# The values of group 6 loaded in two halves, its output rows multiplied ahead of group 7's values, and w4 with ten rows to a partition

## The chip, the cores and the metric

The kernel runs on one core of one Trainium2 chip. The metric is the device time of one execution in microseconds (us), lower being better, as the median of five runs. A profile of one further execution gives the durations of single instructions and the records of the data transfers. Times within the profile are counted from the start of its span.

## The reference, cut to what matters

One token (512 numbers) is normalised. One branch attends with 32 heads over the last 4096 positions of a cache of keys and values; the other is a small feed-forward block. The result is `x + s * g`.

```python
W = min(4096, max(256, Sk // 4))              # 4096
q = (xn @ wq).reshape(...)                    # 32 heads of 128
scores = einsum("bhqd,bhkd->bhqk", q, k[:, :, Sk - W:, :]) * Dh ** -0.5
o = einsum("bhqk,bhkd->bhqd", softmax(scores), v[:, :, Sk - W:, :])
s = o.reshape(1, 1, 32 * 128) @ wo            # wo: 4096 x 512
h2 = gelu(layernorm(x1) @ w3) @ w4            # w3: 512 x 1376, w4: 1376 x 512
g = silu(x1 + h2)                             # with one token the shifted h is zero
out = x + s * g
```

Keys and values of the window are 32 x 4096 x 128 bf16 each, 33.6 MB each; the weights add another 11.7 MB. Every byte is used once.

## The kernel before, in words

The heads are worked in NG = 8 groups of G = 4. A group's keys are one tile of 128 partitions x 128 positions x 128 numbers (4 MB, 32 KB to a partition, loaded by `load_kv` at L97), and its values are another. The main loop (L507) has ten steps. In step s the keys of group s are scored: part of the positions on VectorE (`k_vector`, L297: a product and a sum), the rest turned on TensorE, copied by ScalarE and multiplied on TensorE (`k_turn`, L313, and `k_scores`, L321). The softmax of group s - 1 is ended, and the values of group h = s - 2 are multiplied by its weights (`v_part`, L410, one small matmul for each of the 128 positions of a partition, L423). Steps 8 and 9 have no keys left: step 8 works on the values of group 6, step 9 on those of group 7.

All loads but the two of x are issued by SyncE in program order (`load`, L78). A key tile can be loaded once one of three key buffers is free, a value tile once one of two value buffers is free: the values of group 7 go to the buffer of group 5, and so wait for the multiplication of group 5 (in step 7). Each transfer reports on one of eight semaphores in turn, so that it also waits until the transfer eight before it has landed. On TensorE, VectorE and ScalarE the order in the loop is kept as it is written (`manual_schedule`, L503).

The rows of the output weight `wo` are used in three blocks. Heads 0 to 15 are multiplied in step 6 (`y_wide`), heads 16 to 23 in step 8 (`y_block(1)`). Of heads 24 to 31, which are groups 6 and 7, a first piece is gathered (`few`, block 2): the 20 x 2 rows of `wo_few` (loaded at L395, 160 KB twice) hold 320 of group 6's 512 rows, and need `ox_pick` and `ox_few`, a chain of two matmuls and three VectorE instructions after the values of group 6. The other rows lie in `wo_rows`, one head to a slot, and are multiplied by `y_head` (L498): heads 26 and 27 with group 6 (`h_part` = 26), heads 28 to 31 with group 7. `rows_add` (L147) issues four matmuls for each row column.

In the last step (s = 9, L518 to L522 and L590 to L599) SyncE issues the first rows of `wo_rows`, the values of group 7 in three pieces (positions 0 to 64, 64 to 112 and 112 to 128, `cuts` at L502), and the rows of heads 28 to 31 in three transfers. TensorE multiplies the first piece of group 7's values, then the few block and heads 26 and 27, then the other two pieces of values; VectorE scales the result (`v_out`, L442), TensorE multiplies heads 28 to 31, VectorE multiplies by g and adds x (L602, L604), and SyncE stores 1 KB (L605).

At the start, w4 (1376 rows) is loaded in three transfers (L91 to L93): rows 0 to 1023 with 8 rows to a partition, rows 1024 to 1279 with 2, and the last 96 with one. The columns of w3 that belong to a chunk of w4's rows are picked with the same step (`chunks`, L204 to L206, used at L210 and L221): step 8 for eight chunks, 2 for two chunks, 1 for the last.

## Time and profile before

| what | us |
|---|---|
| median of 5 runs | 194.5 (194.4, 194.5, 194.5, 194.59, 195.68) |
| the profiled execution, whole | 195.93 |
| its span | 194.0 |
| VectorE busy | 145.8 (75%) |
| TensorE matmuls busy | 133.5 (69%) |
| ScalarE busy | 86.0 (44%) |
| the 16 DMA engines, busy on SyncE's queue | 96.0% of the span |
| bytes read | 78.84 MB, 406 GB/s over the span |

The profile shows the busy time of each engine, the transfers by queue, the chain of work that ended last, and a timeline of instructions. A line of the timeline gives start, duration, engine, line of the kernel, operation, output and inputs with their shapes and count; in brackets stands how long the engine had been idle before, and what ended that. "SPq" is SyncE issuing transfers. PEld is TensorE loading weights, which runs beside its matmuls (PE). The granted TensorE clock was 0.67 of full speed in the mean over the span.

### The profile page before, as it was taken

How to read it: one execution, taken by the hardware profiler on the slowest of the kernel's cores; microseconds unless marked ns; L12 is line 12 of the kernel's file. 1: busy time of each engine (PE TensorE's matmuls, PEld its weight loads, DVE VectorE, ACT ScalarE, POOL GpSimd, SP SyncE). 2: the span in 40 equal slices, each digit the busy share in tenths (PEclk: the TensorE clock that was granted, in tenths of full speed). 3: DMA queues.
4: the chain of work that ended last, by engine and by line, in shares of the span. 5: the costliest groups of instructions: out<-in, count | busy, mean ns of one | idle time of the engine just before them, and what ended most of it. 6: DMA issues, size and time to landing. Idle time of an engine off the chain costs nothing.

```text
span 194.0 us, 4716 instructions
## 1 busy us (share of the span) xinstructions
PE 133.5 (69%) x2098; PEld 101.6 (52%) x2098; DVE 145.8 (75%) x160; ACT 86.0 (44%) x193; POOL 6.5 (3%) x14
## 2 busy tenths in 40 slices
PE   0549750987946469878686994981788878843792
PEld 0444540876835433467675444881668246832781
DVE  1540119986999999999999999996799999950201
ACT  2003010788788280367376304771385069740000
POOL 2110007000000000000000000000000000000000
PEclk9999965567575556995555599555555599855555
DMA  5999999999999999999999999999999999999980
GB/s 208 404 408 426 378 422 464 426 432 429 426 442 426 432 427 422 439 432 432 429 429 426 432 429 402 463 432 429 432 429 434 429 432 399 463 411 373 413 333 18
DMA packets 4869, 79.13 MB, mean 408 GB/s; under 512 B 682, under 2 KB 1482, under 8 KB 1866
## 3 DMA queue, kind: packets, MB, share of 16 engines
q1 hardware_dynamic: 4698, 78.84, 96.0%
q8 instruction: 16, 0.26, 0.6%
q10 hardware_dynamic: 152, 0.00, 0.0%
q14 instruction: 3, 0.02, 0.0%
HBM read 78.84 MB, written 0.00 MB: 406 GB/s over the span
## 4 chain that ended last, share of the span: by engine, by line
DVE 42%; DMA 38%; PE 11%; ACT 6%; issue 1%; SPq 0%; ACTq 0%
DMA kv<-in_A_k_cache_dram 27%; DVE S L303 25%; DVE prod L301 14%; DMA kv<-in_A_v_cache_dram 9%; ACT kt L319 5%; PE pt L317 3%; PE yr_ps L489 3%; PE oT L423 3%; DMA x_bf<-in_A_x_dram 2%; PE sT L325 1%; DVE S L339 1%; DVE m L341 1%; DVE mx L349 1%; ACT own L334 0%; SPq L79 0%
## 5 line engine op out<-in xcount | busy, mean ns | idle before, releaser
L303 DVE TENSOR_REDUCE S<-prod 128x20 f32<-128x2560 bf16 (+1 forms) x32 | 83.8, 2620 | 1.1
L319 ACT COPY kt<-pt 128x1024 bf16<-128x1024 bf16 x54 | 53.2, 1014 | 25.7 <-PE pt L317 25.0
L317 PE MATMUL pt<-ident_bf,kv 128*128 128x128 bf16 x432 | 46.2, 277 | 12.0 <-DMA kv<-in_A_k_cache_dram 10.3
L301 DVE TENSOR_TENSOR prod<-kv,q_bc 128x2560 bf16<-128x2560 bf16 (+1 forms) x32 | 44.3, 1386 | 5.6 <-DMA kv<-in_A_k_cache_dram 2.9
L317 PEld LDWEIGHTS <-kv 128*128 128x128 bf16 x432 | 37.1, 127 | 14.3 <-DMA kv<-in_A_k_cache_dram 10.7
L325 PE MATMUL sT<-qT_bf,kt 128*128 128x4 bf16 x432 | 20.1, 169 | 16.5 <-ACT kt L319 15.6
L325 PEld LDWEIGHTS <-kt 128*128 128x128 bf16 x432 | 16.9, 105 | 23.9 <-ACT kt L319 23.7
L423 PE MATMUL oT<-pT,kv 128*128 128x4 bf16 x768 | 21.5, 166 | 3.3 <-DMA kv<-in_A_v_cache_dram 3.1
L423 PEld LDWEIGHTS <-kv 128*128 128x128 bf16 x768 | 21.0, 103 | 5.1 <-DMA kv<-in_A_v_cache_dram 4.8
L415 PE MATMUL ov<-kv,pT 128*16 128x512 bf16 x64 | 18.6, 464 | 0.0
L363 ACT ACTIVATE pT<-S,mb 128x128 bf16<-128x128 f32 x32 | 13.9, 570 | 0.3
L415 PEld LDWEIGHTS <-pT 128*16 128x16 bf16 x64 | 6.6, 105 | 11.1 <-issue 6.3
L442 DVE TENSOR_TENSOR o<-oT,rden 128x4 bf16<-128x4 f32 x2 | 0.3, 163 | 13.8 <-PE oT L423 13.8
L334 ACT ACTIVATE own<-sT,par 128x48 f32<-128x48 f32 (+1 forms) x32 | 7.6, 359 | 3.7 <-PE sT L325 3.7
L363 ACT ACTIVATION_READ_ACCUMULATOR pT<-S,mb 128x1 f32 x32 | 8.2, 255 | 0.0
L446 ACT ACTIVATE o<-oT,rden 128x1 bf16<-128x1 f32 x24 | 4.3, 260 | 8.2 <-PE oT L430 4.6
L418 ACT COPY ov_sb<-ov 16x512 f32<-16x512 f32 x2 | 1.2, 576 | 14.6 <-PE ov L415 14.6
L224 DVE COPY hr<-hr_ps 1x512 f32<-1x512 f32 x1 | 0.7, 679 | 7.7 <-PE hr_ps L221 7.7
L356 PE MATMUL mb_ps<-md,par_t 5*128 5x4 f32 x16 | 4.2, 328 | 2.6 <-DVE md L351 1.9
L489 PE MATMUL yr_ps<-wo,ox 128*1 128x512 bf16 x16 | 5.3, 506 | 0.9 <-DVE ox L467 0.9
L347 PE MATMUL mt_ps<-ident_f,m 128*1 128x128 f32 x8 | 2.9, 360 | 3.8 <-DVE rden L374 3.8
L213 ACT ACTIVATE a_bf<-a_ps 128x10 bf16<-128x10 f32 x1 | 0.2, 180 | 11.9 <-PE a_ps L210 11.9
(113 smaller groups left out, 89.5 us busy)
## 6 DMA issues: line engine op xcount, KB each, us to landing
kv<-in_A_k_cache_dram SPq DMA_DIRECT2D x7, 4096.0 KB, 31.6
kv<-in_A_v_cache_dram SPq DMA_DIRECT2D x7, 4096.0 KB, 30.5
wq_sb<-in_A_wq_dram SPq DMA_DIRECT2D x1, 4096.0 KB, 19.0
kv<-in_A_k_cache_dram SPq DMA_DIRECT2D x2, 2048.0 KB, 24.0
wo<-in_A_wo_dram SPq DMA_DIRECT2D x1, 2048.0 KB, 30.5
kv<-in_A_v_cache_dram SPq DMA_DIRECT2D x1, 2048.0 KB, 14.0
kv<-in_A_v_cache_dram SPq DMA_DIRECT2D x1, 1536.0 KB, 17.0
w_sb<-in_B_w_dram SPq DMA_DIRECT2D x1, 1376.0 KB, 6.7
```

Of the source, the lines that this page charges most:

```text
L301: nc.vector.tensor_tensor(out=prod[:, 0:m, :], in0=kn[:, rows, :], in1=q_bc[:, g:g + 1, :].to_broadcast([P, m, Dh]), op=ALU.mult)
L303: nc.vector.tensor_reduce(out=st[g]["S"][:, rows], in_=prod[:, 0:m, :], axis=AX.X, op=ALU.add)
L317: nc.tensor.transpose(pt[:, c - c0, :], kn[:, c, :], ident_bf[:])
L319: nc.scalar.copy(out=kts[b][:, 0:c1 - c0, :], in_=pt[:, 0:c1 - c0, :])
L325: nc.tensor.matmul(st[g]["sT"][:, c - nd(g), :], lhsT=kt[:, c - c0, :], rhs=qT_bf[:, G * g:G * g + G], start=True, stop=True)
L334: nc.scalar.mul(s["own"][:, 0:m, a], s["sT"][:, 0:m, a], par[:, a:a + 1])
L356: nc.tensor.matmul(mb_ps[:], lhsT=par_t[:].rearrange("k b a -> k (b a)"), rhs=md[:], start=True, stop=True)
L363: nc.scalar.activation(out=s["pT"][:, :, a], in_=s["S"][:], func=ACT.Exp, scale=scale, bias=mb[:, a:a + 1], accum_out=s["sum"][:, a:a + 1])
L415: nc.tensor.matmul(s["ov"][:], lhsT=s["pT"][:, c:c + 4, :].rearrange("p i a -> p (i a)"), rhs=v[:, c:c + 4, :], start=(c == 0), stop=(c == ...
L423: nc.tensor.matmul(s["oT"][:], lhsT=v[:, c, :], rhs=s["pT"][:, c, :], start=(c == 0), stop=(c == CP - 1))
L446: nc.scalar.mul(o_blk[b][:, c + k:c + k + 1], st[g]["oT"][:, k:k + 1], st[g]["rden"][:, k:k + 1])
L489: nc.tensor.matmul(yr[i][:], lhsT=ox_blk[i][:, t:t + 1], rhs=wo_blk[i][:, t, :], start=(t == 0), stop=(t == n - 1))
```

## The change

The second half of the diff splits the load of the values of group 6 (h == NG - 2) into two transfers of 64 positions, 16 KB to a partition each, and puts the few block and heads 26 and 27 before the first piece of group 7's values on TensorE. The first half loads rows 0 to 1279 of w4 in one transfer of 10 rows (10 KB) to a partition instead of two of 8 and 2 rows, and picks w3's columns with step 10 accordingly. Nothing else is changed; the number of SyncE's transfers stays the same, one fewer at the start and one more near the end. Line numbers after L92 move up by one to three.

```diff
-    assert F == 8 * P + 2 * P + 96
+    assert F == 10 * P + 96
...
-    load(w4_sb[:, 0:8, :], B_w4[0:8 * P, :].rearrange("(p c) n -> p c n", p=P))
-    load(w4_sb[:, 8:10, :], B_w4[8 * P:10 * P, :].rearrange("(p c) n -> p c n", p=P))
+    load(w4_sb[:, 0:10, :], B_w4[0:10 * P, :].rearrange("(p c) n -> p c n", p=P))
     load(w4_sb[0:96, 10, :], B_w4[10 * P:F, :])
...
-    chunks = [(P, slice(r, 8 * P, 8)) for r in range(8)]
-    chunks += [(P, slice(8 * P + r, 10 * P, 2)) for r in range(2)]
+    chunks = [(P, slice(r, 10 * P, 10)) for r in range(10)]
     chunks += [(96, slice(10 * P, F, 1))]
...
         elif h >= 0:
-            v = load_kv(v_pool, A_v_cache, h)
+            v = load_kv(v_pool, A_v_cache, h, (0, 64, CP) if h == NG - 2 else (0, CP))
...
         else:
-            v_part(h, v, 0, cuts[1])
             y_block(few_block)
             for r in range(h_part, H - G):
                 y_head(r)
-            for c0, c1 in zip(cuts[1:], cuts[2:]):
+            for c0, c1 in zip(cuts, cuts[1:]):
                 v_part(h, v, c0, c1)
             v_out(h)
```

## The prediction

> **What bounds the kernel now.** I read the page's slices first, then the transfers by queue, then the end of the chain of waits, and last the timeline of the last 15 us.

> ```profile
> DVE  1540119986999999999999999996799999950201
> DMA  5999999999999999999999999999999999999980
> GB/s 208 404 408 426 378 422 464 426 432 429 426 442 426 432 427 422 439 432 432 429 429 426 432 429 402 463 432 429 432 429 434 429 432 399 463 411 373 413 333 18
> ...
> q1 hardware_dynamic: 4698, 78.84, 96.0%
> q8 instruction: 16, 0.26, 0.6%
> ```

> VectorE is 75% busy, but its nines end near slice 35 (170 us). The DMA row is at nine from the second slice to the last but one. From 33 to 170 us the windows view gives a DMA share of 1.00 and 430 GB/s. In the trace's records of single packets, 16 are in flight at nearly every sampled moment from 3 to 186 us. So the transfers are never short of issued work: the bound is 78.84 MB through 16 engines.

> ```profile
> 170.62 0.15 SPq L79
> 170.77 0.04 issue
> 170.82 16.99 DMA kv<-in_A_v_cache_dram
> 187.81 0.05 issue
> 187.85 1.88 PE oT L423 x64
> 189.73 0.02 issue
> 189.76 0.17 DVE o L442
> 189.93 0.04 issue
> 189.97 0.72 PE y_ps L150 x15
> ```

> The chain shows the end: the second piece of group 7's values lands at 187.81, 64 small matmuls follow, VectorE scales, heads 28 to 31 are multiplied. But it hides one wait. The records of landings put the last row of wo (head 31) at 190.34, and the single records of L150 show its four matmuls starting at 190.39. So the very last transfer releases the end; the chain through 187.81 ends at almost the same moment. After 190.39 there are 3.66 us of span: a matmul, two VectorE instructions, a store, the program's end.

> ```profile
> 174.20 1.02 PE L150 MATMUL y_ps<-wo,ox 128*1 128x128 bf16 x32 [0.62 <-DVE ox L467]
> 175.15 0.60 PE L150 MATMUL y_ps<-y_row,ones_f 1*1 1x128 f32 x8
> 178.86 3.58 PE L423 MATMUL oT<-pT,kv 128*128 128x4 bf16 x128 [3.11 <-DMA kv<-in_A_v_cache_dram]
> 184.17 0.16 DVE L476 CAST of<-of_ps 64x8 bf16<-64x8 f32 x1 [0.26 <-PE of_ps L473]
> 184.22 1.87 PE L423 MATMUL oT<-pT,kv 128*128 128x4 bf16 x64
> 186.02 1.02 PE L150 MATMUL y_ps<-wo_few,of 64*1 64x128 bf16 x32
> 187.85 1.87 PE L423 MATMUL oT<-pT,kv 128*128 128x4 bf16 x64
> 190.72 0.29 DVE L602 TENSOR_TENSOR y<-y_ps,g_row 128x128 f32<-128x128 f32 x1 [0.80 <-PE y_ps L150]
> ```

> To be seen here: TensorE waits for group 6's values until 178.86, for the first piece of group 7 until 184.22, and for the second until 187.85. Between these it has slack.

> [...] one row's landings spread from 186.5 to 190.34 us, and each half of `few` (20 partitions) has five data landings[...]. [...] q8 above has 16 such packets, of 1.00 to 1.14 us each[...].

> **The change part by part.**

> *Group 6 in halves.* The bytes stay; 128 packets of 32 KB become 256 of 16 KB. From the packet records: 32 KB takes 1.213 us at the median (1.228 mean), 16 KB 0.614 (0.637 with the instruction packets among them). Per engine 16 x 0.614 - 8 x 1.213 = +0.12 us at the medians; with both minima (0.611 and 1.213) +0.07. The dearest price the trace offers is that of group 7's first piece, 0.652 in its window: 16 x 0.652 - 8 x 1.229 = +0.60. Below zero there is no reason. I take +0.08, and it is on the path. SyncE issues one more transfer (0.53 to 0.6 us); queued behind it are two wo_rows loads and group 7's. These are not delayed, since group 7's issue waits for group 5's multiplication until 170.2, and the queue of work then lasts until 178.8, a cover of 8.6 us.

> TensorE's first half can start when it lands. The last engine gets there about 16 KB x 8 = 4.9 us before 178.8, so at 173.9; TensorE is free at 175.75. 64 matmuls at 27.3 ns end at 177.5, the second half runs from 178.9 to 180.7 instead of 182.4. `of` (184.33 before, 1.9 us after the last of these matmuls) is ready at 182.6. That is 1.7 us earlier, on a chain that nothing late waits for.

> *Output rows first.* The 32 + 8 matmuls (1.02 us and some 0.65 us) run from 182.6 to 184.3. The first piece of group 7, landed at 184.17, then runs 184.3 to 186.2. Next is the second piece, which lands at 187.81 plus the 0.08: TensorE idles 1.7 us instead of 0.36 and starts at the same moment. Gain zero: what was filled with row matmuls becomes a wait. If the halves brought nothing, `of` would stay at 184.33, the rows end at 186.1, the first piece at 188.0, and the 64 matmuls behind it at 189.8: 0.1 us late. In both orders the third piece (landed 189.03) is done by 189.8.

> *w4 in one transfer.* 8 KB takes 0.309 us, 2 KB 0.084, 11,008 bytes 0.413; 10 KB is not in the trace. Between 8 KB and 11,008 bytes it comes to 0.385: 8 x (0.385 - 0.393) = -0.07 us per engine. The ends are 8 x (0.413 - 0.393) = +0.16 and, at the 11,008-byte rate scaled, -0.07. I take -0.07. One issue less on SyncE (0.43 us) leaves all later ones earlier, which a full queue doesn't notice. The columns of w3 are picked with step 10 instead of 8 or 2: L210's weight loads take 103 to 311 ns, 44 of them. If all took 311, it would be 13.7 us instead of 2.6. Even these 11 us would hide: SyncE would issue the first values at some 40 instead of 28.7 us, when two groups of keys are in the queue until 52.9. The first keys would be scored later by up to 6 us, and the transfers behind have covers of 8.6 us and more. I take zero.

> *Waits by turn.* The transfer eight places before has to have landed before the next is issued. The shifted count changes the partners. The second half of group 6 waits for group 6's keys (landed 136.8), a wo_rows load for group 7's keys (156.2 instead of 151.9), the pieces of group 7 for group 5's values (166.0) and wo loads up to 168.5: all before 170.2, when group 7's buffer comes free. The last two rows wait for the two halves of group 6, at the latest 178.8 as now.

> Sum on the path: +0.08 - 0.07 + 0 + 0 = 0.0 us on a profiled execution of 195.93 (span 194.0, 1.9 around it). The other runs, at a median of 194.5, lie 1.4 below the profiled one; I carry the difference of zero over to 194.5.

> **The rivals.**

> *A (forecast): the transfers bound it and nothing moves.* For it: the full DMA row and the landing at 190.34 just before 190.39. 194.5, with the bounds above 194.4 to 195.2. Chance 0.60, all of it within 0.5%, which is 0.97 us and about what a measurement of this kernel can tell from no change.

> *B (slower): the last engine is made later by a packet of another queue.* Landings of the last row: 3 engines by 186.9, one at 188.2, the other 12 between 189.0 and 190.34. Instruction packets of 1.0 to 1.14 us come at 178.3, 184.8 and 188.7. TensorE now runs row matmuls and values in another order and earlier, so these fetches come at other moments. It decides from the point at which a fetch meets an engine that would land the last row after about 190.2 without it: then the end is 1.1 us later, 195.6. For it: one run of before is 195.68, 1.2 above the others. Against it: the number of fetches is the same, and which engine gets one need not depend on the moment. Chance 0.22.

> *C (faster): the late engines are relieved.* If the fetches, or the shorter w4 packets, fell so that all engines ended together, the last row would land at the mean of the 16 landings, about 189.0, and the end would come 1.3 us earlier: 193.2. More isn't there, since the bytes are the same. Against it: four engines and more are within 0.35 us of the last, and all would have to be relieved. Chance 0.12.

> *D (faster, by the order alone): multiplying group 6 earlier shortens the tail by its 1.7 us*, 192.8. For it, the chain runs through TensorE at the end. Against it, group 7's second piece and the last row are awaited in any case. Chance 0.06.

> **How the numbers follow.** Predicted 194.5. A's own range is 194.0 to 195.2; B adds 195.6 and a little over it, C reaches down to 193.2. 193.3 to 195.8 leaves out D, and the outer parts of B and C, less than 2 in 10. Faster 0.12 + 0.06 = 0.18, same 0.60, slower 0.22.

> **What would show it.** In the profile after: the DMA row again at nine to the last slice but one; the last row landing within 0.3 us of 190.34; group 6's matmuls in two runs, the first near 175.8; the row matmuls of wo_few near 182.6; the idle time before group 7's second piece at about 1.7 us for the values; L602 near 190.7. I am wrong if the DMA row shows a gap (an issue held up by its partner), if 16 KB packets take over 0.65 us, if the landing of the last row moves by a microsecond, or if the time after it isn't 3.7 us.

## The result, and the profile after

The changed kernel takes 196.57 us at the median of 20 runs (195.36 to 198.28), the kernel before 194.56 of 39. The ratio is 1.0089 (95% interval 1.0070 to 1.0109): slower by about 0.9%, where no change was forecast. The profiled execution took 195.62 (span 193.7), at the low end of the changed kernel's times; the one profiled before lies, with 195.93, at the high end of its own, so the two traces side by side don't show the loss.

From the page of the changed kernel, the slices of the transfers and the transfers by queue:

```profile
DMA  5999999999999999999999999999999999999970
GB/s 202 418 491 433 386 419 460 408 426 430 433 423 433 433 435 430 433 433 433 430 436 426 433 430 416 450 433 430 433 430 428 430 433 386 433 427 405 424 270 0
...
q1 hardware_dynamic: 4698, 78.84, 95.5%
q8 instruction: 16, 0.26, 0.5%
```

The transfers are as full as before and end earlier: the last slice but one moves 270 GB/s instead of 333, and the last row of wo lands at 189.16 by the landing records, against 190.34 in the profile of before. So the time isn't lost there. The end of the chain of waits tells where it is lost:

```profile
183.42 1.61 PE oT L421 x57
185.03 2.45 issue
187.49 2.05 PE oT L421 x71
189.56 0.17 DVE o L440
189.73 0.04 issue
189.78 0.62 PE y_ps L149 x16
```

Before, the chain came here from the landing of group 7's second piece. Now it comes from TensorE itself: after 57 of the 64 matmuls on the first piece it stands still for 2.45 us, and the profile finds nothing that it waited for ("issue"). The second piece had landed at 186.68, 0.8 us before TensorE went on. The timeline of the changed kernel (start, duration, what, and in brackets the idle time before and what ended it) has a second such stop earlier:

```profile
174.63 1.87 PE L421 MATMUL oT<-pT,kv 128*128 128x4 bf16 x64
177.71 1.17 PE L421 MATMUL oT<-pT,kv 128*128 128x4 bf16 x38 [1.21 <-DMA kv<-in_A_v_cache_dram]
179.30 0.85 PE L421 MATMUL oT<-pT,kv 128*128 128x4 bf16 x26 [0.41 <-issue]
182.10 1.02 PE L149 MATMUL y_ps<-wo_few,of 64*1 64x128 bf16 x32 [0.25 <-DVE of L474]
183.36 1.68 PE L421 MATMUL oT<-pT,kv 128*128 128x4 bf16 x57
187.49 2.04 PE L421 MATMUL oT<-pT,kv 128*128 128x4 bf16 x71 [2.45 <-issue]
190.43 0.29 DVE L599 TENSOR_TENSOR y<-y_ps,g_row 128x128 f32<-128x128 f32 x1 [0.70 <-PE y_ps L149]
```

Group 6's halves and the rows run in the order that the prediction gave them, 0.5 to 1.2 us earlier. What TensorE lacks at the stops seems to be its own instructions. Count its records in order of time, weight loads, matmuls and the 14 of semaphores and drains alike: the four longest stops in the middle of a run of matmuls that no wait for a semaphore explains (0.9, 2.2, 0.6 and 2.6 us from start to start), at the 450th, 1730th, 3778th and 4034th, lie multiples of 256 apart, and each ends 1.3 to 1.4 us after the end of the transfer of one of the 16 instruction packets (q8, 16 KB each). I read that as a block of 256 instructions which TensorE reaches before it has come. Counted on from the 450th in steps of 256, borders and packets pair off in order (the last packet is for a border behind the program's end), and in none of the 19 profiles of this case did the first instruction of a block run less than 1.2 us after the end of its packet. The records of before have the stop at the 4034th too: 0.42 us among the rows of heads 26 and 27, where the wait for group 7's second piece covered it.

Theory T1, for the experiments: in the tail TensorE reaches a block early, and what stands behind the stop ends the kernel. T2: the 16 KB packets of the halves cost transfer time. T3: w4's new transfer, or w3's columns with step 10, cost time.

### The profile page after: what moved, and what is told of

It reads as the page before. It is cut to its first block, busy times and chain, and to the rows that moved or that the text cites. A ratio compares the mean times of both kernels' runs of the same rounds, so it can differ in the third digit from the quotient of the medians.

```text
span 193.7 us, 4715 instructions
## 1 busy us (share of the span) xinstructions
PE 135.3 (70%) x2098; PEld 103.4 (53%) x2098; DVE 145.9 (75%) x160; ACT 86.0 (44%) x193; POOL 6.5 (3%) x14
## 3 DMA queue, kind: packets, MB, share of 16 engines
q1 hardware_dynamic: 4698, 78.84, 95.5%
HBM read 78.84 MB, written 0.00 MB: 407 GB/s over the span
## 4 chain that ended last, share of the span: by engine, by line
DVE 42%; DMA 29%; PE 19%; issue 5%; ACT 3%; POOL 1%; SPq 0%; POOLq 0%; ACTq 0%
DVE S L301 24%; DMA kv<-in_A_v_cache_dram 14%; DVE prod L299 13%; DMA kv<-in_A_k_cache_dram 12%; PE oT L421 5%; PE pt L315 3%; PE hr_ps L219 2%; DMA x_bf<-in_A_x_dram 2%; PE qT_ps L235 2%; ACT kt L317 2%; PE a_ps L208 1%; PE y_ps L149 1%; PE sT L323 1%; PE hr_ps L216 1%; PE oT L428 1%
## 5 line engine op out<-in xcount | busy, mean ns | idle before, releaser
L315 PE MATMUL pt<-ident_bf,kv 128*128 128x128 bf16 x432 | 46.7, 280 | 8.7 <-DMA kv<-in_A_k_cache_dram 6.8
L315 PEld LDWEIGHTS <-kv 128*128 128x128 bf16 x432 | 37.8, 129 | 11.0 <-DMA kv<-in_A_k_cache_dram 7.1
L421 PEld LDWEIGHTS <-kv 128*128 128x128 bf16 x768 | 21.2, 103 | 5.3 <-issue 3.6
L413 PE MATMUL ov<-kv,pT 128*16 128x512 bf16 x64 | 17.2, 436 | 0.0
L428 PE MATMUL oT<-ident_f,ov_sb 16*128 16x4 f32 x16 | 3.1, 314 | 4.5 <-DVE rden L372 4.5
```

Of the source, the lines that this page charges most:

```text
L315: nc.tensor.transpose(pt[:, c - c0, :], kn[:, c, :], ident_bf[:])
L413: nc.tensor.matmul(s["ov"][:], lhsT=s["pT"][:, c:c + 4, :].rearrange("p i a -> p (i a)"), rhs=v[:, c:c + 4, :], start=(c == 0), stop=(c == ...
L421: nc.tensor.matmul(s["oT"][:], lhsT=v[:, c, :], rhs=s["pT"][:, c, :], start=(c == 0), stop=(c == CP - 1))
L428: nc.tensor.matmul(s["oT"][:], lhsT=s["ov_sb"][:, j, :], rhs=ident_f[0:4 * G, G * j:G * j + G], start=(j == 0), stop=(j == 3))
```

## The experiments

**The parts alone.** The order alone (e1):

```diff
-            v_part(h, v, 0, cuts[1])
             y_block(few_block)
...
-            for c0, c1 in zip(cuts[1:], cuts[2:]):
+            for c0, c1 in zip(cuts, cuts[1:]):
```

> The order alone: few block and heads 26 and 27 ahead of the first values of group 7; group 6 in one load and w4 in two loads as before. Theory T1 (in the tail TensorE waits for its next block of 256 instructions, and the order decides which work stands behind that wait): with group 6 in one load the block before is entered as late as before (about 181 us), the next block is wanted inside group 7's first values, and what comes late by the fetch delays the end: 195.0 to 196.6. Rival T2 (the 16 KB packets of the halves cost transfer time): 194.5. Rival T3 (w4 with ten rows to a partition costs): 194.5.

Measured: 194.88, ratio 1.0014 (0.9990 to 1.0038). The stop is where T1 puts it, but short:

```profile
184.41 1.68 PE L423 MATMUL oT<-pT,kv 128*128 128x4 bf16 x57
186.45 2.03 PE L423 MATMUL oT<-pT,kv 128*128 128x4 bf16 x71 [0.36 <-issue]
```

TensorE goes on at 186.45, before the second piece lands (186.56). So the place of the stop isn't enough; T1 had forecast a loss here, and missed.

The halves alone (e2):

```diff
-            v = load_kv(v_pool, A_v_cache, h)
+            v = load_kv(v_pool, A_v_cache, h, (0, 64, CP) if h == NG - 2 else (0, CP))
```

> Group 6 in two halves alone. T1: TensorE enters the block of 256 instructions inside group 6's values some 2 us earlier and waits for the next one among the row matmuls of heads 26 and 27, where the wait for group 7's second piece covers it: 194.3 to 194.8. T2 (packets): slower by what the whole change costs, about 196.5. T3 (w4): 194.5.

Measured: 194.71, ratio 0.9993 (0.9972 to 1.0014). The stop inside group 6's values is there, and costs nothing:

```profile
179.76 0.85 PE L423 MATMUL oT<-pT,kv 128*128 128x4 bf16 x26 [0.83 <-issue]
183.08 1.87 PE L423 MATMUL oT<-pT,kv 128*128 128x4 bf16 x64 [0.77 <-DMA kv<-in_A_v_cache_dram]
186.71 1.87 PE L423 MATMUL oT<-pT,kv 128*128 128x4 bf16 x64 [0.51 <-DMA kv<-in_A_v_cache_dram]
```

w4 alone (e3):

```diff
-    load(w4_sb[:, 0:8, :], B_w4[0:8 * P, :].rearrange("(p c) n -> p c n", p=P))
-    load(w4_sb[:, 8:10, :], B_w4[8 * P:10 * P, :].rearrange("(p c) n -> p c n", p=P))
+    load(w4_sb[:, 0:10, :], B_w4[0:10 * P, :].rearrange("(p c) n -> p c n", p=P))
...
-    chunks = [(P, slice(r, 8 * P, 8)) for r in range(8)]
-    chunks += [(P, slice(8 * P + r, 10 * P, 2)) for r in range(2)]
+    chunks = [(P, slice(r, 10 * P, 10)) for r in range(10)]
```

> w4 with ten rows to a partition alone. T1 and T2: 194.5, within 0.2. T3 (the shape of the w4 transfer, or columns of w3 picked with step 10): about 196.5.

Measured: 195.0, ratio 1.0001 (0.9973 to 1.0029). T2 and T3 fall: neither the packets nor w4 cost anything that shows.

**The pair, and the change again.** Halves and order without w4 (e5, the diffs of e1 and e2 together), and the changed kernel unaltered (e6):

> Halves and order together, w4 in two transfers as before. If the loss is the pair's own (T1: group 6's early values and the rows put TensorE at the start of its next block, inside group 7's first values, before the block has come): 196.2 to 197.0, as the whole change. If w4's transfer has a part in it after all (one transfer fewer ahead of all others), though alone it costs nothing: 194.5 to 195.2.

> The changed kernel unaltered, for a second profile and a time in the same round of runs. T1: 196 to 197, and TensorE stands still inside group 7's first values before the 4034th of its records, until 1.2 to 1.5 us after an instruction packet's end, later than 187.5 where the run is slower than the profiled one of before. Rival (the wait was an accident of one profile, and the loss is in the transfers): no such wait, the last row landing about 191.

Measured: 196.26, ratio 1.0061 (1.0036 to 1.0086), and 196.24, ratio 1.0069 (1.0045 to 1.0093). The loss is the pair's. In the timeline of e6:

```profile
180.28 0.85 PE L421 MATMUL oT<-pT,kv 128*128 128x4 bf16 x26 [1.52 <-issue]
184.34 1.68 PE L421 MATMUL oT<-pT,kv 128*128 128x4 bf16 x57
188.47 2.04 PE L421 MATMUL oT<-pT,kv 128*128 128x4 bf16 x71 [2.45 <-issue]
190.76 0.59 PE L149 MATMUL y_ps<-wo_rows,o 128*1 128x128 bf16 x16 [0.25 <-DVE o L440]
```

The last row had landed at 189.02 and the second piece at 186.48; the final matmuls start at 190.76, 2.0 us later than in e1 (188.74), whose span is 1.9 shorter. So the loss in time is the loss in TensorE. The other profiles say the same: in the kernel before, e1 to e4 and every later run without the loss, the last four matmuls start 0.04 to 0.05 us after the landing of the last row; in the changed kernel it is 0.9, in e5 1.6 and in e6 2.0 us.

**Moving the blocks.** If the blocks are the cause, added instructions far ahead, in idle time, must change the time by where they put the blocks' beginnings. The added matmuls write zeros into the output's accumulator before anything is added to it:

```diff
-    rows_open(y_ps)
+    for _ in range(39):
+        rows_open(y_ps)
```

That is e4 (38 matmuls more, 76 instructions); e8, e10, e11 and e12 have 16, 1, 8 and 24 more, and e7 adds 59 to the kernel before.

> The changed kernel with 38 more matmuls (76 TensorE instructions, zeros into the output's accumulator before anything is added to it) in TensorE's idle time near the start. They move every later instruction by 76 places against the blocks of 256, so that one block now begins with the second half of group 6's values, at a wait for data, and the next 20 matmuls into group 7's first values. T1: the block is asked for 1.6 us earlier, the end comes earlier: 194.5 to 195.8. T2 and T3: 196.6 as the changed kernel, or later by the added matmuls.

> The changed kernel with 16 more matmuls (32 TensorE instructions) near the start: the block that comes late begins 16 matmuls earlier within group 7's first values, so that 0.4 us more work stands behind it, and it is asked for about 0.4 us earlier. T1: 196 to 197.2, no gain. Rival (any matmuls added near the start, [...]bring the gain that the 76 instructions brought): 195.

> The changed kernel with one more matmul near the start: the blocks begin two instructions earlier. If the loss belongs to where the block begins: 196.0 to 196.8, as the changed kernel. If it hangs on an accident of timing or layout of the very program: anything, 194.6 as likely.

> The changed kernel with 8 more matmuls near the start (16 instructions), halfway to the 32 that took the loss away. If the loss goes gradually with the place: 195.2 to 195.8. If there is an edge: near 196.4 or near 194.7.

> The changed kernel with 24 more matmuls near the start (48 instructions), between the 32 that gave 194.68 and the 76 that gave 195.03: 194.5 to 195.0. A candidate for a version at least as fast as the kernel before, if the block begins at a place where the waits for data cover it.

| instructions added | median us | ratio to before |
|---|---|---|
| 2 (e10) | 194.65 | 0.9984 (0.9961 to 1.0008) |
| 16 (e11) | 194.49 | 0.9982 (0.9965 to 0.9999) |
| 32 (e8) | 194.68 | 0.9987 (0.9965 to 1.0008) |
| 48 (e12) | 194.48 | 0.9989 (0.9974 to 1.0004) |
| 76 (e4) | 195.03 | 1.0004 (0.9987 to 1.0020) |

All of them take the loss away, e8 and e10 against the forecasts that went with T1: a shift by a single matmul is enough. In e10's timeline the same work stands in the same order, and the second stop is 0.39 instead of 2.45 us:

```profile
179.87 0.88 PE L422 MATMUL oT<-pT,kv 128*128 128x4 bf16 x27 [1.00 <-issue]
183.96 1.65 PE L422 MATMUL oT<-pT,kv 128*128 128x4 bf16 x56
186.00 0.35 PE L422 MATMUL oT<-pT,kv 128*128 128x4 bf16 x8 [0.39 <-issue]
186.67 1.87 PE L422 MATMUL oT<-pT,kv 128*128 128x4 bf16 x64 [0.32 <-DMA kv<-in_A_v_cache_dram]
```

Was it the place of the blocks, or any added matmul? Three runs part these: e13 adds 128 matmuls of one column near the start, a whole block, so that every place stays; e14 adds 127, which moves the beginnings by two instructions the other way; e15 adds one matmul behind the late block's beginning.

```diff
+    for _ in range(128):
+        nc.tensor.matmul(y_ps[:, 0:1], lhsT=zero_bf[:], rhs=ident_bf[:, 0:1], start=True, stop=False,
+                         skip_group_check=True)
     rows_open(y_ps)
```

```diff
+            nc.tensor.matmul(y_ps[:], lhsT=zero_bf[:], rhs=ident_bf[:], start=False, stop=False,
+                             skip_group_check=True)
             v_out(h)
             for r in range(H - G, H):
```

> The changed kernel with 128 matmuls of one column (256 TensorE instructions, one whole block, some 3.5 us of idle time) near the start: all later instructions keep their place within a block. If the place within the block makes the loss: 196.0 to 196.8, and the block inside group 7's first values is again asked for about 5.8 us before its transfer starts. If it hangs on the count of blocks or on any added matmul: 194.4 to 194.9.

> The same with 127 matmuls (254 instructions), so that every block begins two instructions later in the program's text than in the changed kernel, not two earlier as with one matmul. If the edge is at the exact place: 194.5 to 195.2. If the late block is a range of places that ends where one matmul earlier begins: 196.0 to 196.8.

> The changed kernel with one matmul of zeros added after group 7's values, behind the late block's beginning: nothing before it moves. If the one matmul of the earlier run helped by shifting the blocks: 196.0 to 196.8 here. If one instruction more anywhere helps: 194.5 to 194.9.

Measured: e13 196.69, ratio 1.0094 (1.0070 to 1.0119); e14 196.06, ratio 1.0069 (1.0043 to 1.0095); e15 196.6, ratio 1.0085 (1.0062 to 1.0107). The same place gives the same loss with 256 instructions more, and one matmul more behind the place helps nothing. The place within the block decides, with an edge between neighbouring matmuls: the places of the changed kernel and of e14 lose, that of e10 doesn't.

The stop can also be set on the kernel before, with nothing of the change in it (e7):

> The kernel before with 59 more matmuls (118 TensorE instructions) in the idle time near the start, chosen so that a block of 256 begins with the last two of group 7's value matmuls, and the block before inside its first piece. T1: asked for at about 184, the block comes 5.7 us later, at 189.5, one microsecond after it is wanted: 195.3 to 196.3, slower than before, though nothing of the change is in it. Rival (blocks don't matter; the added matmuls lie in idle time): 194.5 to 194.8.

Measured: 195.6, ratio 1.0027 (1.0007 to 1.0047). The sign is as forecast, the size at the lower end by the medians. The stop stands where it was put, ahead of the last two value matmuls:

```profile
186.57 1.82 PE L424 MATMUL oT<-pT,kv 128*128 128x4 bf16 x62 [0.29 <-DMA kv<-in_A_v_cache_dram]
189.24 0.19 PE L424 MATMUL oT<-pT,kv 128*128 128x4 bf16 x2 [0.84 <-issue]
```

Here the block's transfer starts only 2.7 us after the entry of the block before; the stop is shorter than in the changed kernel, and the last four matmuls start 0.9 us after the last row's landing.

**What makes the block late.** Worked out from the records of TensorE and of the instruction packets: when the block inside group 6's values is entered, how long after that the transfer of the next block starts, and for how long TensorE then stands ahead of it (from start to start of neighbouring instructions).

```
kernel                     entered   transfer starts after   standstill
before                      181.57          3.25                0.42
e1  order alone             180.35          3.65                0.53
e2  halves alone            179.76          3.55                none
e10 change + 2 instr.       179.86          3.76                0.55
change                      179.29          5.83                2.62
e5  halves + order          179.90          5.84                2.62
e6  change again            180.27          5.88                2.61
e15 late matmul             179.98          5.86                2.61
e13 a whole block more      180.90          5.95                2.62
e14 127 matmuls more        180.45          5.92                2.62
```

A transfer took 1.0 us (1.05 in the kernel before, 1.01 in the changed one), and where TensorE stood waiting the block ran 1.3 to 1.5 us after it. In the slow kernels the transfer starts 2.1 to 2.7 us later after the entry than in the others. Two readings were tried against a fixed delay from the entry. Does it start only when TensorE has run dry? e9 puts four long matmuls, whose result nothing reads, ahead of group 7's first values:

```diff
+            idle_ps = ps_tr.tile([1, D], FP32, tag="pt", name="idle_ps")
+            for t in range(4):
+                nc.tensor.matmul(idle_ps[:], lhsT=zero_bf[:, 0:1], rhs=wo_blk[1][:, t, :], start=True,
+                                 stop=True)
             for c0, c1 in zip(cuts, cuts[1:]):
```

> The changed kernel with four matmuls of 512 columns (about 1.7 us, 8 instructions, into an accumulator that nothing reads) between the rows of heads 26 and 27 and group 7's first values. It parts two readings of the late block, which in three profiles came 8.2 us after the block before it had been entered. If the transfer starts a fixed 5.85 us after that entry: TensorE's standstill inside group 7's first values shrinks from 2.6 to about 1.1 us, and the time stays at 196.0 to 196.6. If the transfer starts only when TensorE has run out of instructions: the standstill stays at 2.6 us and all comes 1.5 us later, 197.5 to 198.5. If no block matters (rival), the 1.7 us fit into the wait for group 7's second piece or add at most 0.5.

Measured: 196.22, ratio 1.0057 (1.0031 to 1.0083). The added work costs nothing that shows in the time. It lengthens the stretch ahead of the stop by 1.7 us, and the standstill shrinks from 2.6 to 1.6 us (start to start; 1.1 was forecast), so that the late block runs 8.7 us after the entry of the one before instead of 8.2:

```profile
183.42 1.91 PE L594 MATMUL idle_ps<-wo,zero_bf 128*1 128x512 bf16 x4
185.27 1.57 PE L421 MATMUL oT<-pT,kv 128*128 128x4 bf16 x53
188.25 2.14 PE L421 MATMUL oT<-pT,kv 128*128 128x4 bf16 x75 [1.41 <-issue]
```

The transfer started at 185.69, 1.1 us before TensorE ran dry, 6.19 after the entry. Does it wait for the rows' matmuls, which start 3.05 us ahead of it? e20 makes these later by an unused VectorE product ahead of `of`:

```diff
+        slow = prod_pool.tile([P, 20, Dh], BF16, tag="prod", name="slow")
+        nc.vector.tensor_tensor(out=slow[:, 0:16, :].rearrange("p a b -> p (a b)"),
+                                in0=wo_blk[1][:, 0:4, :].rearrange("p a b -> p (a b)"),
+                                in1=wo_blk[1][:, 4:8, :].rearrange("p a b -> p (a b)"), op=ALU.mult)
         of = sm_pool.tile([64, 8], BF16, tag="of", bufs=1, name="of")
```

> The changed kernel with one VectorE product (128 x 2048 bf16, about 1.2 us, its result unused) ahead of the instruction that makes `of`, so that the rows' matmuls start about 1.0 us later after the entry of the block. If the next block's transfer starts a fixed 5.85 us after that entry: TensorE's standstill inside group 7's first values shrinks from 2.6 to about 1.6 us, the time stays at 196.2 to 196.8. If it starts some 3.05 us after the wait for `of` ends (as it did in seven profiles): the standstill stays at 2.6, the start moves to 6.9 us after the entry, and the time rises to 197.0 to 197.8.

Measured: 196.43, ratio 1.0088 (1.0056 to 1.0120), within the first reading's range; the standstill is 1.8 us.

```profile
183.18 1.02 PE L149 MATMUL y_ps<-wo_few,of 64*1 64x128 bf16 x32 [1.04 <-DVE of L478]
184.44 1.68 PE L421 MATMUL oT<-pT,kv 128*128 128x4 bf16 x57
187.78 2.03 PE L421 MATMUL oT<-pT,kv 128*128 128x4 bf16 x71 [1.67 <-issue]
```

The rows start 3.6 us after the entry (2.8 in the changed kernel), and the transfer again 5.80 after it. So in these two runs the delay follows the entry of the block (6.19 and 5.80 us), or something close behind it, and not the rows or running dry. Why it is 5.8 to 6.2 us at this place stays open. At most other borders it is 2 to 5 us, but the place in the tail isn't the only one: e4 and e12 have a delay of 6.6 and 6.4 us one block earlier, ahead of a stop inside group 6's values, and lose no time by it. The entry is also only near the moment that counts, since at some borders far ahead the transfer started before the first record of the block (3.0 us before the 1986th record of the changed kernel).

**The change with the blocks out of its way.** e11 again (e21):

> The changed kernel with 8 more matmuls near the start again, the fastest of the shifted ones (194.49 against 194.72, an interval that just left out 1): 194.3 to 194.7; its ratio tells whether the change, with the blocks out of its way, gains at all. If it gains: below 0.9995 again. If not: 1 within the interval.

Measured: 194.41, ratio 0.9985 (0.9963 to 1.0008), after 0.9982 (0.9965 to 0.9999) the first time. A gain of 0.15% is possible and not shown: no version clearly beats the kernel before.

## Why the prediction was wrong

- *Transfers bound it and are unchanged*: right. The row of the transfers is full, 10 KB packets took 0.385 us as interpolated, and the last row landed at 189.02 to 189.23 in the changed kernel, e6 and e13, as in e1 (189.07). It wasn't within 0.3 us of 190.34, because the execution profiled before was itself a late one.
- *The halves' price of +0.08 us, w4's -0.07, the waits by turn free*: nothing in e2 and e3 contradicts it; each part alone measures zero within 0.3%.
- *"TensorE idles 1.7 us instead of 0.36 and starts at the same moment. Gain zero"*: this is the step that failed. It let TensorE wait for data only. In the changed kernel it waits, as I read the stops, for its instructions: 0.6 to 1.7 us inside group 6's values and 2.6 us inside group 7's first values, by the records of the changed kernel and e6. The second piece's matmuls stand behind that, and instead of 1.7 us of slack there are up to 2.0 us of loss (e6 against e1).
- *The earlier half*: worked as said, but that TensorE is earlier isn't what costs. In e6 it enters the block inside group 6 at 180.27 and has used it up at 186.0; in e1, with the order alone, at 180.35 and 186.1. What differs is the transfer of the next block, 5.88 us after the entry in e6 and 3.65 in e1. In all eight profiles with the late transfer in the tail TensorE had stood still for 0.6 to 2.3 us at the border before; the kernel before and e1, with group 6 in one load, have no stop there. But e2, e8, e10 and e11 have such a stop, of 0.3 to 1.2 us, and no late transfer. So the pair costs because it makes the block late; why it does is not shown.
- *Rival B* (slower) named the instruction packets, but as a delay of the data on one engine, at 195.6. No late landing was found in the changed kernel. As I read the stops, the packets matter as TensorE's supply: in the changed kernel four stops end 1.3 to 1.4 us after one.
- The range ended at 195.8 and the median is 196.57: the bounds were those of transfers and of the end's order, and no bound stood for the supply of instructions to TensorE. The profile of before had offered one: "issue" as a releaser of TensorE, and stops of 1.2 and 2.0 us at the 450th and 1730th record.

So a border cost TensorE up to 2.6 us here (the changed kernel, e5, e6 and e13 to e15), and in the tail what stood behind it ended the kernel.

## What to carry to other kernels

In this kernel TensorE, with 4196 weight loads and matmuls, stood still for up to 2.6 us for what I read as a want of instructions. Where an engine runs hundreds of short instructions, look for idle time that nothing ended, and count in which instruction it falls. Two edits that were free alone (ratios 1.0014 and 0.9993) cost 0.6% together (1.0061); between them they moved what stood at a block's border and when TensorE got there. A few idle instructions added far ahead test such a cause, and may cure it; since here a single matmul more made the difference, a cure of this kind should be taken to hold for this program only.
